# Seeds of a Vandermonde product: factors made at another copy, phases rounded against a constant in PSUM, seeds laid out by power

## The chip, the core and the metric

One core of a Trainium2 chip runs the whole kernel. The core has five engines that each take their instructions in order and wait for one another by semaphores: PE (matmuls; its weight loads are listed apart as PEld), DVE (vector work), ACT (activations and copies), POOL (a second elementwise engine) and SP, which here issues all DMAs. SBUF is the memory on the chip, PSUM the smaller one that PE writes its products to.

The metric is the device time of one execution in microseconds (us), lower is better. Before the change it was 1309.37 us (median of three runs, 1307.53 to 1311.9).

## The reference

Two independent layers read their own inputs; their outputs are joined on the last axis.

```python
# A: a diagonal state space layer, L = 2048, D = 448, N = 256
dt = jnp.exp(log_dt)
A = -jnp.exp(log_A_real) + 1j * A_imag
C = (C_real + 1j * C_imag) * dt[:, None]
P = jnp.exp((A * dt[:, None])[:, :, None] * pos[None, None, :])     # pos = 0 ... 2047
K = 2.0 * jnp.einsum("dn,dnl->dl", C, P).real
y = irfft(rfft(u_t, 2 * L) * rfft(K, 2 * L))[:, :, :L]              # a causal convolution
a = y.transpose(0, 2, 1) + u * D_skip

# B: attention with 16 heads of 28
qkv = (x @ wqkv).reshape(B, S, 3, 16, 28).transpose(2, 0, 3, 1, 4)
p = softmax(q @ k^T * 28 ** -0.5)
b = (p @ v).transpose(0, 2, 1, 3).reshape(B, S, 448) @ wo

out = concatenate([a, b], axis=-1)
```

K[d, l] is a sum over 256 modes of C z^l with z = exp(A dt). The kernel writes l = 64 n1 + n2: per channel it needs two tables of powers of z, called e (64 powers) and g (32 powers, with C in them), and K is their product, summed over the modes on PE.

## The kernel before, in words

The program has two parts.

**The seeds stage** (0 to 239 us of the profile). PE makes q, k and v from x in float32r with a high and a low half. Beside it the function `seeds(o)` (line 314) works through eight groups o of seven channel blocks each: it loads the parameters (`nat`), multiplies them by dt, turns them so that modes lie on partitions (`turn`, into a PSUM tile `pn`), forms 15 multiples of each phase (`phases`: r on DVE, mg on POOL, both 128 x 1680), reduces the phases to half a turn by adding and subtracting a large constant MAGIC (`reduce`: sn = round(r), then r = sn - r), takes sines and cosines on ACT (`sines`) and sizes with Exp (`sizes`), and makes from them: the seeds of e (eight low powers; `places` sets the power 0, `e_all` the others on POOL, into a tile named qhat), the seeds of g (four low powers) and, for each block, the parts of the factors by which the tables are later doubled. All go out to DRAM as `sd`. The list of stages returned at the end of `seeds` is laid over slots, four slots per group; inside this part a scheduler may put instructions of an engine in another order than they are written in.

The tables of ACT hold either Exp or Sin, so a change between them costs a table load (ACT_TABLE_LOAD).

**The loop** (239 to 1275 us): 256 steps, 16 per unit of queries. Here every engine keeps the order in which the program was written. `ORDER` (line 34) sets one step out by hand: m0 to m3 are four products of the row maxima for the unit after (`max_mm`: m0 goes to ACT, m1 to 3 to DVE, which writes mx), s0 to s3 the scores of four heads (`s_mm`, tile pss; ACT takes Exp to p), pv the product with v (tile po), f a slot for other work, v one entry of DVE's queue, k the bookkeeping of the channel blocks, w a slot for wide work. The products of m and f share a ring of three PSUM tiles (pm), so PE can go on only when DVE or ACT has read the one three before.

The 56 channel blocks run through the loop beside attention:

- `load_sd(b)` loads a block's seeds (`sdb`), three blocks ahead.
- `k_seeds(b)` (line 605) is called twice: ACT copies the seeds of e into the table e, some steps later those of g into the table g.
- `k_factors(b)` (line 615): three DVE instructions of 128 x 96 (`fz<-sdb`) multiply sizes by cosines and sines.
- `k_begin` (line 976) starts block b when its due time `K0 + b * KP` (KP = 3.5 steps) has passed and both queues of powers are empty. It copies part of fz into PSUM (`zg`, on ACT) and fills the queues: nine POOL instructions that double e three times (`e_power`, three a step; tiles e and eu), nine entries for DVE that double g (`g_powers`), and a tenth, the factors of block b + 1. DVE takes three entries a step, one of them after k in the step's order.
- From four steps after the start, three f slots multiply e and g (`pm<-e,g`, then `pm<-w,ko`) and send the result to DRAM.

From step 192 on, f slots also run the spectrum: 16 jobs "s" (products with `mw`, elementwise products on DVE, sums on POOL in the tile p, back to DRAM as z), of which the last eight need all 56 blocks, and eight jobs "f" (load zi and ut, `skip` on POOL, four products each, addition on DVE, output). What is left of them behind the last step is interleaved with the last unit's projection. SP issues all loads and stores in program order; a store waits there for its data, and what stands behind it waits too.

Of the kernel before, what the change touches and what calls it, by code (L numbers as in the profile page):

```python
# [8 lines left out]
F32 = mybir.dt.float32  # L9
F32R = mybir.dt.float32r  # L10
I32 = mybir.dt.int32
AF = mybir.ActivationFunctionType
ALU = mybir.AluOpType
# [11 lines left out]
CQ = 512  # L25
# [25 lines left out]
NB = D // 8  # L51
# [3 lines left out]
PO = BO * 8  # L55
LV = 15
NF, NE = 6, 13
F_G = 256
# [3 lines left out]
MAGIC = 1.5 * 2 ** 23  # L62
# [29 lines left out]
def body(ctx, tc, a, out):  # L92
    nc = Engines(tc)
# [4 lines left out]
    def pool(stack, name, bufs=1, space=None, side=None):  # L98
        kw = {} if space is None else {"space": space}
        if side:  # L100
            kw["side"] = side
        return stack.enter_context(tc.tile_pool(name=name, bufs=bufs, reuse_waits="tile", **kw))
# [110 lines left out]
    with ExitStack() as st:  # L213
# [7 lines left out]
        ps_n = pool(st, "ps_n", 2, PSUM)  # L221
# [39 lines left out]
        t = a["A_log_dt"]  # L261
# [6 lines left out]
        half_pi = s_p.tile([128, 1], F32, name="half_pi")  # L268
# [42 lines left out]
        NH = BO * 16  # L311
        mul = lambda e, o_, x_, y_: e.tensor_tensor(o_, x_, y_, ALU.mult)

        def seeds(o):

            q = {}
            vec, pol, act = nc.vector, nc.gpsimd, nc.scalar
# [6 lines left out]
            def times_dt(i):  # L324
                n, d = q["nat"][:, i, :], dt_all[:, i or 4, o:o + 1]
                act.activation(n, n, AF.Copy, scale=d)

            def turn():
                q["ps"] = ps = ps_n.tile([128, CQ], F32, name="pn")[:, :8 * PO].rearrange("p (a b h e) -> p a b h e", a=4, h=2, e=8)
                for i in range(4):  # L330
                    for h in range(2):
                        nc.tensor.transpose(ps[:, i, :, h, :], q["nat"][:, i, h * 128:(h + 1) * 128], ident[:PO, :PO])
                q["tr"] = s_p.tile([128, NH], F32, name="tr", bufs=2)
                act.activation(q["tr"], ps[:, 0].rearrange("p b h e -> p (b h e)"), AF.Copy)
# [10 lines left out]
                mul(pol, mg, lb(q["tr"]), kb(1))  # L345

            def reduce():
                vec.tensor_scalar(q["sn"], q["r"], MAGIC, MAGIC, op0=ALU.add, op1=ALU.subtract)
                vec.tensor_tensor(q["r"], q["sn"], q["r"], ALU.subtract)

            def places():
                se = q_p.tile([128, HG, CQ], F32R, name="qhat", bufs=3).bitcast(F32).rearrange("p h q -> p (h q)")
                q["se"] = se = se[:, :BO * F_G].rearrange("p (b f) -> p b f", f=F_G)
                q["e8"] = se.rearrange("p b (c h e) -> p b c h e", c=2, e=8)
                pol.memset(q["e8"][:, :, 0, :, 0], 1.0)
                pol.memset(q["e8"][:, :, 1, :, 0], 0.0)

            def g_place():
                q["sg"] = sg = s_p.tile([128, BO, SDF - F_G], F32, name="sg", bufs=SGB)
# [15 lines left out]
                both(q["mg"], 0, AF.Exp)  # L375

            def e_all():
                ev = lambda t: t[:, NF:NE].rearrange("p e (b h) -> p b h e", h=16)
                for c, t in enumerate(("r", "sn")):
                    mul(pol, q["e8"][:, :, c, :, 1:], ev(q["mg"]), ev(q[t]))  # L380

            def g_base():

# [29 lines left out]
            def load():  # L413
                if o not in nats:
                    load_nat(o)
                q["nat"] = nats.pop(o)
            dts = lambda *r: [lambda i=i: times_dt(i) for i in r]
            return [[load], [exp_a] + dts(1, 2, 3), dts(0), [turn], [phases], [g_place, reduce], [sines], [sizes, places, g_base],
                    [e_all, g_first], [put_e], [g_copies], [], [put_g]]

        xh, xl = {}, {}
# [177 lines left out]
    sds, egs = {}, {}  # L599
# [5 lines left out]
    def k_seeds(b):  # L605

        if b not in es:
            es[b] = e = g_p.tile([128, 2, 16, N2], F32, name="e", bufs=2)
            nc.scalar.activation(e[:, :, :, :8], sds[b][:, :F_G].rearrange("p (c h e) -> p c h e", c=2, e=8), AF.Copy)
        else:  # L610
            g = g_p.tile([128, 2, 16, N1], F32, name="g", bufs=2)
            nc.scalar.activation(g[:, :, :, :4], sds[b][:, F_G:F_Z].rearrange("p (c h e) -> p c h e", c=2, e=4), AF.Copy)
            egs[b] = es.pop(b), g

    def k_factors(b):
        fzs[b] = fz = g_p.tile([128, 3, 6 * 16], F32, name="fz", bufs=2)
        mg, cs, sn = (sds[b][:, F_Z + 96 * i:F_Z + 96 * i + 96] for i in range(3))
        nc.vector.tensor_tensor(fz[:, 0], mg, cs, ALU.mult)
        nc.vector.tensor_tensor(fz[:, 2], mg, sn, ALU.mult)
        nc.vector.scalar_tensor_tensor(fz[:, 1], mg, -1.0, sn, op0=ALU.mult, op1=ALU.mult)  # L620

    def k_start(b):
        zgs[b] = ps_g.tile([128, CQ], F32, name="zg")
        nc.scalar.activation(zgs[b][:, :Z_G].rearrange("p (f n) -> p f n", f=3), fzs[b][:, :, 48:], AF.Copy)

    def e_power(b, i, q):

        t, m = egs[b][0], 8 << i
        zz = fzs[b].rearrange("p f (k h) -> p k f h", k=6)
        if q == 0:  # L630
            zr = zz[:, i, 0, :][:, None, :, None].to_broadcast([128, 2, 16, m])
            nc.gpsimd.tensor_tensor(t[:, :, :, m:2 * m], t[:, :, :, :m], zr, ALU.mult)
        elif q == 1:
            uts[0] = g_p.tile([128, 2, 16, 32], F32, name="eu")[:, :, :, :m]
            zi = zz[:, i, 1:3, :][:, :, :, None].to_broadcast([128, 2, 16, m])
            nc.gpsimd.tensor_tensor(uts[0], t[:, ::-1, :, :m], zi, ALU.mult)
        else:
            nc.gpsimd.tensor_tensor(t[:, :, :, m:2 * m], t[:, :, :, m:2 * m], uts[0], ALU.add)

    def g_powers(b):  # L640

        t, zg = egs[b][1], zgs[b]
        zz = zg[:, :Z_G].rearrange("p (f k h) -> p k f h", k=3, f=3)
        tt = nc.vector.tensor_tensor

        def first(i, m):
            tt(t[:, :, :, m:2 * m], t[:, :, :, :m], zz[:, i, 0, :][:, None, :, None].to_broadcast([128, 2, 16, m]), ALU.mult)

        def second(i, m, c):
            n = c.stop - c.start  # L650
            u = zg[:, CQ // 2:CQ // 2 + n * 16 * m].rearrange("p (c h m) -> p c h m", c=n, m=m)
            zi = zz[:, i, 1 + c.start:1 + c.stop, :][:, :, :, None].to_broadcast([128, n, 16, m])
            tt(u, t[:, ::-1, :, :m][:, c], zi, ALU.mult)
            return lambda: tt(t[:, c, :, m:2 * m], t[:, c, :, m:2 * m], u, ALU.add)
        both, u = slice(0, 2), {}

        def lowest():
            first(0, 4)
            second(0, 4, both)()
        ops = [lowest, lambda: first(1, 8), lambda: u.update(a=second(1, 8, both)), lambda: u["a"](), lambda: first(2, 16)]  # L660
        for c in (slice(0, 1), slice(1, 2)):
            ops += [lambda c=c: u.update(a=second(2, 16, c)), lambda: u["a"]()]
        return ops
# [196 lines left out]
        max_mm(1, 0, kc)  # L860
    for _ in range(2):
        k_seeds(0)
    k_factors(0)

    urgent, back = collections.deque(), collections.deque()
    powers = {"g": collections.deque(), "e": collections.deque()}
# [109 lines left out]
    def k_begin(s_):  # L976
        if not (k_due and K0 + k_due[0] * KP <= s_ and k_due[0] in egs and not powers["e"] and not powers["g"]):
            return
        b = k_due.popleft()
        k_start(b)  # L980
        powers["g"] += g_powers(b)
        if b + 1 < NB:
            powers["g"].append(lambda: k_factors(b + 1))
        powers["e"] += [lambda i=i, q=q: e_power(b, i, q) for i in range(3) for q in range(3)]
        p0, p1, p2 = k_mm(b)

        def m1():
            p1()
            done["mm"] = b
        m_due.extend((s_ + KD + i, t_) for i, t_ in enumerate((p0, m1, p2)))  # L990
        last[0] = b
# [15 lines left out]
    for s in range(NS):  # L1007
# [26 lines left out]
        ps = []  # L1034
        for op in ORDER:
            if op[0] == "s":
                ps.append(s_mm(u, kt, int(op[1])))
            elif op[0] == "f":
                slot(s)
            elif op == "w":  # L1040
                wide_slot()
            elif op[0] == "v":
                vec()
            elif op == "k":
                k_next()
                k_begin(s)
                for _ in range(1 if s else 2):
                    k_seed(s)
                for _ in range(3):
                    if powers["e"]:  # L1050
                        powers["e"].popleft()()
            elif op == "pv":
                if prev:
                    pv_step(*prev)
                    if prev[1] == NK - 1:
                        fin(prev[0], s)
            elif sm < NS:
                max_mm(sm // NK, sm % NK - more, int(op[1]))
# [80 lines left out]
```

## Time and profile before

| what | us |
|---|---|
| median of three runs (lowest, highest) | 1309.37 (1307.53, 1311.9) |
| the profiled execution, its own time | 1310.93 |
| its span, first to last instruction | 1308.8 |
| PE busy in the span | 1225.8 (94%) |
| DVE busy | 948.6 (72%) |
| ACT busy | 963.7 (74%) |
| POOL busy | 839.0 (64%) |
| granted TensorE clock, mean | 0.98 |

How its lines are read. "L76" stands on every line, since one helper at line 76 records all instructions; the tiles tell them apart. A group reads: line, engine, operation, tile written <- tiles read, partitions x elements written <- read, xcount | busy us, mean ns of one | idle us of the engine just before them, and what ended it. A line of the timeline has start and length in us, engine, operation, tiles, shape and count, then idle time before it. A line of windows has the stretch, its length, busy us of PE, PEld, DVE, ACT and POOL (with the number of instructions), the granted clock, the busy share of the DMA engines and GB/s. A line of waits has the waiting and the awaited engine and tile, us in total, times, and the longest. The chain of waits goes back from the last instruction to what released it, step by step.

### The profile page before, as it was taken

How to read it: one execution, taken by the hardware profiler on the slowest of the kernel's cores; microseconds unless marked ns; L12 is line 12 of the kernel's file. 1: busy time of each engine (PE TensorE's matmuls, PEld its weight loads, DVE VectorE, ACT ScalarE, POOL GpSimd, SP SyncE). 2: the span in 40 equal slices, each digit the busy share in tenths (PEclk: the TensorE clock that was granted, in tenths of full speed). 3: DMA queues.
4: the chain of work that ended last, by engine and by line, in shares of the span. 5: the costliest groups of instructions: out<-in, count | busy, mean ns of one | idle time of the engine just before them, and what ended most of it. 6: DMA issues, size and time to landing. Idle time of an engine off the chain costs nothing.

```text
span 1308.8 us, 32327 instructions
## 1 busy us (share of the span) xinstructions
PE 1225.8 (94%) x12177; PEld 686.0 (52%) x12177; DVE 948.6 (72%) x2194; ACT 963.7 (74%) x2048; POOL 839.0 (64%) x656
## 2 busy tenths in 40 slices
PE   6888976899999999999999999999999999999996
PEld 5666853455555555555555555555555555454332
DVE  5676678878877887777788888888888958453221
ACT  4878873588888888888878888888877657565451
POOL 2455641467777787777788888878879849235341
PEclk9989988899999999999999999999999999999998
DMA  6777779546864545487524225431454533269577
GB/s 195 230 255 267 260 235 294 157 93 153 183 151 105 126 147 167 112 215 196 155 71 95 74 51 136 109 96 39 109 151 124 171 99 107 82 187 287 170 228 192
DMA packets 200084, 205.30 MB, mean 157 GB/s; under 512 B 95992, under 2 KB 158520, under 8 KB 197880
## 3 DMA queue, kind: packets, MB, share of 16 engines
q1 hardware_dynamic: 199928, 203.24, 55.3%
q8 instruction: 96, 1.57, 0.5%
q14 instruction: 60, 0.49, 0.1%
HBM read 120.74 MB, written 82.18 MB: 155 GB/s over the span
## 4 chain that ended last, share of the span: by engine, by line
PE 71%; DVE 8%; DMA 4%; POOL 4%; ACT 3%; issue 2%; SPq 1%; POOLq 0%; DVEq 0%; ACTq 0%
PE pm L76 40%; PE pss L76 16%; PE po L76 16%; DVE mx L76 2%; DMA ut<-in_A_u 2%; POOL p L76 1%; DVE rl L76 1%; ACT tri L76 1%; DVE tri L76 1%; POOL e L76 1%; SPq L76 1%; DVE pr L76 1%; DVE mh L76 1%; ACT sg L76 1%; DVE fz L76 1%
## 5 line engine op out<-in xcount | busy, mean ns | idle before, releaser
L76 ACT ACTIVATE p<-pss 128x512 f32<-128x512 f32 x1024 | 561.9, 610 | 127.9 <-PE pss L76 125.7
L76 DVE TENSOR_REDUCE mx<-pm 128x1 f32<-128x512 f32 x500 | 321.7, 684 | 128.7 <-PE pm L76 127.6
L76 PE MATMUL pss<-qhat,khat 128*128 128x512 f32 x1024 | 403.0, 400 | 0.7 <-ACT p L76 0.6
L76 PE MATMUL pm<-khat,qhat 128*128 128x512 f32 x749 | 330.3, 443 | 9.6 <-DVE mx L76 6.8
L76 POOL TENSOR_TENSOR e<-e,fz 128x256 f32<-128x256 f32 x168 | 203.2, 1209 | 202.3 <-PE pss L76 84.0
L76 PE MATMUL po<-p,v 128*32 128x512 f32 x2048 | 269.8, 594 | 0.0
L76 PEld LDWEIGHTS pm<-khat,qhat 128*128 128x128 f32 x749 | 141.5, 189 | 220.1 <-DVE mx L76 41.5
L76 POOL TENSOR_TENSOR e<-e,eu 128x256 f32<-128x256 f32 x168 | 247.9, 1475 | 13.2
L76 PEld LDWEIGHTS pss<-qhat,khat 128*128 128x128 f32 x1024 | 190.5, 189 | 40.3 <-issue 9.6
L76 POOL TENSOR_TENSOR eu<-e,fz 128x256 f32<-128x256 f32 x168 | 201.7, 1200 | 0.0
L76 DVE CUSTOM_DVE_ANT_0 rl<-pm,rl 128x512 f32<-128x512 f32 x249 | 170.8, 686 | 31.6 <-ACT rl L76 27.3
L76 ACT ACTIVATE rl<-pm 128x512 f32<-128x512 f32 x249 | 151.0, 606 | 19.3 <-PE pm L76 18.9
L76 DVE TENSOR_TENSOR g<-g,zg 128x128 f32<-128x128 f32 x392 | 162.1, 413 | 3.6
L76 POOL TENSOR_TENSOR p<-pr,pr 64x448 f32<-64x448 f32 x64 | 73.3, 1146 | 96.9 <-PE pm L76 61.7
L76 PE MATMUL pm<-xh,khat 112*128 112x512 f32 x256 | 89.0, 430 | 20.6 <-DVE kb L76 7.8
L76 PE MATMUL pm<-kdif,qhat 128*128 128x512 f32 x249 | 102.2, 410 | 4.4 <-DVE pr L76 2.2
L76 DVE TENSOR_TENSOR zg<-g,zg 128x128 f32<-128x128 f32 x224 | 87.7, 392 | 4.7
L76 PEld LDWEIGHTS pm<-e,g 128*32 128x32 f32 x3584 | 58.2, 109 | 45.6 <-issue 23.5
L76 DVE TENSOR_TENSOR pr<-pm,ub 128x448 f32<-128x448 f32 x64 | 36.9, 619 | 53.5 <-PE pm L76 38.7
L76 ACT ACTIVATE y<-pm 128x448 f32<-128x448 f32 x48 | 26.3, 547 | 66.9 <-PE pm L76 44.7
L76 PE MATMUL pm<-e,g 128*32 128x64 f32 x3584 | 73.1, 221 | 1.9 <-POOL e L76 1.9
L76 PEld LDWEIGHTS po<-p,v 128*32 128x32 f32 x2048 | 55.1, 110 | 31.8 <-issue 27.7
(129 smaller groups left out, 1435.6 us busy)
## 6 DMA issues: line engine op xcount, KB each, us to landing
sdb<-sd SPq DMA_DIRECT2D x56, 336.0 KB
khat<-k SPq DMA_DIRECT2D x64, 256.0 KB
qhat<-q SPq DMA_DIRECT2D x64, 256.0 KB
sd<-sg SPq DMA_DIRECT2D x8, 1456.0 KB
k<-hl SPq DMA_DIRECT2D x16, 512.0 KB
q<-hl SPq DMA_DIRECT2D x16, 512.0 KB
v<-v SPq DMA_DIRECT2D x32, 256.0 KB
mw<-in_mw SPq DMA_DIRECT2D x16, 512.0 KB
```

The costliest lines, as they stand in the source:

```text
L76: i = f(*args, **kw)
```

## The change

Four edits.

1. `reduce`: sn is now made by an instruction with a second tensor, a constant MAGIC broadcast from one column of the PSUM tile pn, in place of two immediate constants. The column is written by a small DVE instruction in `turn`.
2. The seeds of e lie in their tile by part (cosine, sine), power and mode, where they lay by part, mode and power. `places`, `e_all` and the copy in `k_seeds` follow.
3. The list of stages: exp_a moves two stages later, the other multiplications by dt accordingly, turn and phases share a stage.
4. `k_factors(b)` is called in `k_seeds` directly after the copy of g's seeds, and is no longer the tenth entry of DVE's queue (nor called ahead of the loop).

```diff
             def turn():
-                q["ps"] = ps = ps_n.tile([128, CQ], F32, name="pn")[:, :8 * PO].rearrange("p (a b h e) -> p a b h e", a=4, h=2, e=8)
+                pn = ps_n.tile([128, CQ], F32, name="pn")
+                q["ps"] = ps = pn[:, :8 * PO].rearrange("p (a b h e) -> p a b h e", a=4, h=2, e=8)
+                q["magic"] = pn[:, 8 * PO:8 * PO + 1]
+                vec.tensor_scalar(q["magic"], half_pi, 0.0, MAGIC, op0=ALU.mult, op1=ALU.add)
...
             def reduce():
-                vec.tensor_scalar(q["sn"], q["r"], MAGIC, MAGIC, op0=ALU.add, op1=ALU.subtract)
+                vec.scalar_tensor_tensor(q["sn"], q["r"], MAGIC, q["magic"][:, :, None].to_broadcast([128, LV, NH]),
+                                         op0=ALU.add, op1=ALU.subtract)
                 vec.tensor_tensor(q["r"], q["sn"], q["r"], ALU.subtract)
...
-                q["e8"] = se.rearrange("p b (c h e) -> p b c h e", c=2, e=8)
-                pol.memset(q["e8"][:, :, 0, :, 0], 1.0)
-                pol.memset(q["e8"][:, :, 1, :, 0], 0.0)
+                q["e8"] = se.rearrange("p b (c e h) -> p c e b h", c=2, e=8)
+                pol.memset(q["e8"][:, 0, 0], 1.0)
+                pol.memset(q["e8"][:, 1, 0], 0.0)
...
             def e_all():
-                ev = lambda t: t[:, NF:NE].rearrange("p e (b h) -> p b h e", h=16)
+                ev = lambda t: t[:, NF:NE].rearrange("p e (b h) -> p e b h", h=16)
                 for c, t in enumerate(("r", "sn")):
-                    mul(pol, q["e8"][:, :, c, :, 1:], ev(q["mg"]), ev(q[t]))
+                    mul(pol, q["e8"][:, c, 1:], ev(q["mg"]), ev(q[t]))
...
-            return [[load], [exp_a] + dts(1, 2, 3), dts(0), [turn], [phases], [g_place, reduce], [sines], [sizes, places, g_base],
+            return [[load], dts(1, 2, 3), [], [exp_a] + dts(0), [turn, phases], [g_place, reduce], [sines], [sizes, places, g_base],
                     [e_all, g_first], [put_e], [g_copies], [], [put_g]]
...
             es[b] = e = g_p.tile([128, 2, 16, N2], F32, name="e", bufs=2)
-            nc.scalar.activation(e[:, :, :, :8], sds[b][:, :F_G].rearrange("p (c h e) -> p c h e", c=2, e=8), AF.Copy)
+            nc.scalar.activation(e[:, :, :, :8], sds[b][:, :F_G].rearrange("p (c e h) -> p c h e", c=2, e=8), AF.Copy)
         else:
             g = g_p.tile([128, 2, 16, N1], F32, name="g", bufs=2)
             nc.scalar.activation(g[:, :, :, :4], sds[b][:, F_G:F_Z].rearrange("p (c h e) -> p c h e", c=2, e=4), AF.Copy)
             egs[b] = es.pop(b), g
+            k_factors(b)
...
     for _ in range(2):
         k_seeds(0)
-    k_factors(0)
...
         powers["g"] += g_powers(b)
-        if b + 1 < NB:
-            powers["g"].append(lambda: k_factors(b + 1))
         powers["e"] += [lambda i=i, q=q: e_power(b, i, q) for i in range(3) for q in range(3)]
```

In the built program the starts of the 56 blocks stand in steps 0, 4, 8 ... 220 before the change, and in steps 0, 4, 7, 11, 14, 18, 21 ... 193 after it; the number of table loads goes from 19 to 17.

## The prediction

> **What bounds the kernel now.** I read the busy time of each engine by stage first, then the same stretches for the scores alone, then waits and the timeline where the change acts.
>
> ```profile
> core 0: us, PE busy (x) PEld busy (x) DVE busy (x) ACT busy (x) POOL busy (x), PEclk, DMA share, GB/s
> 0.00:239.00 239.00, 188.17 (x775) 140.26 (x775) 160.75 (x281) 159.85 (x273) 101.45 (x78) 0.91 0.77 247
> 239.00:652.90 413.90, 411.11 (x4398) 219.59 (x4399) 327.92 (x818) 342.31 (x784) 298.74 (x235) 1.00 0.59 149
> 652.90:963.20 310.30, 307.22 (x3356) 169.64 (x3354) 273.38 (x689) 260.37 (x583) 256.60 (x200) 1.00 0.36 85
> 963.20:1275.50 312.30, 298.35 (x3385) 148.25 (x3385) 181.41 (x395) 196.86 (x403) 175.94 (x141) 1.00 0.53 165
> 1275.50:1308.80 33.30, 20.94 (x268) 8.29 (x268) 5.15 (x14) 4.33 (x8) 6.28 (x3) 0.87 0.73 195
> ```
> ```profile
> 239.00:652.90 413.90, 165.16 (x416) 78.90 (x417) 227.81 (x415) 1.00 0.59 149
> 652.90:963.20 310.30, 138.96 (x353) 66.29 (x352) 193.09 (x353) 1.00 0.36 85
> ```
>
> The second fence is the pss tile alone: four matmuls a step, so 416 and 352 are 104 and 88 steps, 3.98 and 3.53 us each. Three regimes follow. The seeds stage (0 to 239) has no full engine; PE idles 239 - 188.2 = 50.8 us on latency chains. The loop to 963 is PE's: 718 of 724 us busy. After it PE idles 13.9 us in the loop's last 64 steps and 12.4 us behind it. So a gain must come from the first stage, from the end, or not at all; a loss can come anywhere in the middle, where DVE has only (413.9 - 327.9)/104 = 0.83 and (310.3 - 273.4)/88 = 0.42 us idle a step.
>
> **The change, part by part.** *Rounding.* The stage's large instructions, grouped by shape:
>
> ```profile
> L76 DVE TENSOR_SCALAR tri<-tri 128x1680 f32<-128x1680 f32 x8 | 15.7, 1968 | 0.1
> L76 DVE TENSOR_TENSOR tri<-pn,pw 128x1680 f32<-128x1680 f32 x8 | 15.2, 1897 | 0.1
> L76 POOL TENSOR_TENSOR tri<-tr,pw 128x1680 f32<-128x1680 f32 x8 | 24.0, 2998 | 8.1 <-issue 5.8 <-ACT tr L76 2.3
> L76 POOL TENSOR_TENSOR qhat<-tri 128x784 f32<-128x784 f32 x16 | 51.1, 3198 | 0.0
> L76 ACT ACTIVATE e<-sdb 128x256 f32<-128x256 f32 x56 | 24.6, 439 | 3.6 <-DMA sdb<-sd 3.6
> L76 ACT ACTIVATE yk<-pm 128x256 f32<-128x256 f32 x56 | 39.3, 701 | 1.5 <-PE pm L76 1.5
> L76 ACT ACT_TABLE_LOAD x19 | 24.4, 1283 | 1.0 <-PEq L1129 0.7
> ```
> ```profile
> 94.67 1.03 DVE L76 TENSOR_SCALAR tri<-tri 128x1680 f32<-128x1680 f32 x1
> ...
> 173.75 7.64 DVE L76 TENSOR_SCALAR tri<-tri 128x1680 f32<-128x1680 f32 x1
> ```
> ```profile
> 174.05 3.01 POOL L76 TENSOR_TENSOR tri<-tr,pw 128x1680 f32<-128x1680 f32 x1
> 177.01 0.66 POOL L76 TENSOR_TENSOR tri<-tri 128x224 f32<-128x224 f32 x1
> 177.63 2.87 POOL L76 TENSOR_TENSOR qhat<-tri 128x784 f32<-128x784 f32 x1
> ```
> ```profile
> 137.72 3.11 POOL qhat L76
> 149.21 1.28 ACT L76
> 173.75 7.64 DVE tri L76
> 183.68 4.61 PE pm L76 x12
> ```
>
> The rounding takes 1.03 us beside an idle POOL and 7.64 us when POOL runs three instructions back to back: it ends at 181.39, after POOL's last one (180.50). The last fence is the chain of waits: that 7.64 lies on it, with PE's projections behind. The new instruction has an operand in PSUM; the nearest row is the product with pn in PSUM, 1.90 us, never longer. That costs 0.87 us where POOL was quiet and saves 5.7 at the stall. DVE is not full here, so of the dear ones I charge one to the path: -5.7 + 0.9 = -4.8. Bounds: the stall only moves to the subtraction behind it, which still has both inputs in SBUF (+1), or a second chain shortens too (-7).
>
> [...]
>
> *Seeds of e.* POOL takes 3.20 us for 784 elements written 8 apart and read 112 apart, and 3.00 for 1680 contiguous ones. Laid out by power, 784 should cost 784 x 3.00/1680 = 1.40 us (bounds 1.4 and 3.2). It saves 16 x 1.8 = 29 us of POOL, of which one, 1.7 us at 137.72, lies on the chain. The copy of these seeds on ACT now reads 16 elements apart: between 0.44 us (its row) and 0.70 (yk, also 256 elements, written in another order). I take 0.44, as ACT idles 50 of 310 us; the other end is 56 x 0.26 = 14.7 us of ACT.
>
> *Stages.* The built program has 17 table loads for 19; one of 1.28 us lies on the chain at 149.21: -1.3. The small write of the constant, eight times, hides beside PE's transposes. The scheduler sorts this stage anew, which no row prices: I add nothing and keep +10/-8. Sum of the stage: -4.8 - 1.7 - 1.3 = -8, range -16 to +6.
>
> *Factors.* DVE's queue per block loses its tenth entry (the factors), so nine remain at three a step. In the built order blocks start at steps 0, 4, 7, 11, 14 ... 193 and no longer at 0, 4, 8 ... 220: every 3.5 steps. Same work, earlier. Its price is where the factors now stand: in the step before a block starts, ahead of two mx reduces that give PE its buffers back, while POOL still works on the block before.
>
> ```profile
> 810.27 0.41 DVE L76 TENSOR_TENSOR fz<-sdb 128x96 f32<-128x96 f32 x2
> ...
> 810.78 0.68 DVE L76 CUSTOM_DVE_ANT_0 rl<-pm,rl 128x512 f32<-128x512 f32 x1
> ...
> 821.35 0.69 DVE L76 CUSTOM_DVE_ANT_0 rl<-pm,rl 128x512 f32<-128x512 f32 x1 [0.20 <-ACT rl L76]
> ```
> ```profile
> 810.69 0.66 POOL L76 TENSOR_TENSOR e<-e,fz 128x256 f32<-128x256 f32 x1 [2.52 <-ACT rl L76]
> ...
> 820.22 2.38 POOL L76 TENSOR_TENSOR e<-e,eu 128x1024 f32<-128x1024 f32 x1
> ```
> ```profile
> 653.45 2.33 POOL L76 TENSOR_TENSOR e<-e,eu 128x1024 f32<-128x1024 f32 x1
> 653.67 2.40 DVE L76 TENSOR_TENSOR fz<-sdb 128x96 f32<-128x96 f32 x2
> ```
> ```profile
> 980.70 1.34 DVE L76 TENSOR_TENSOR fz<-sdb 128x96 f32<-128x96 f32 x2
> 981.97 1.20 DVE L76 SCALAR_TENSOR_TENSOR fz<-sdb 128x96 f32<-128x96 f32 x1
> ```
>
> At 810 the factors take 0.6 us together because POOL has finished and waits for them (it starts 0.42 us after). At 653 and 980 POOL is busy, and they wait for its instruction to end: 2.0 us there, and 2.5 us from first to last here, for 0.6. Now POOL's run takes 810.69 to 822.60, 11.9 us, so it is busy until 12.3 us after the factors that start it. From one rl of a step to that three steps on (810.78 to 821.35) pass 10.6 us. With blocks three steps apart the next factors meet POOL's last instruction with 1.75 us left, 1.6 us more than now; four steps apart (14.1 us) POOL is done. So one block in two waits 1.6 us. DVE's own idle swallows 0.4. From step 104 to 193 there are 89/7 = 12.7 such pairs: 12.7 x 1.2 = +15 us. Before step 104 three steps take 11.9 us, the wait is 0.4, and DVE's 0.83 idle covers it: 0. Bounds: +4 (a third is felt) and +38 (the first rival).
>
> [...]
>
> *The last part of the loop.* Eight blocks leave the stretch from 963; there PE waited for mx behind such factors (the waits from 963 to 1116: us, times, longest):
>
> ```profile
> PE pm L76 <- DVE mx L76: 4.4, 8, 0.7
> ```
>
> With them POOL's mixture of e and p goes too. Of 13.9 us idle I take back 6 (0 to 10).
>
> *The end.*
>
> ```profile
> 1293.04 1.35 SPq L76 DMA_DIRECT2D ut<-in_A_u  x2
> ...
> 1293.90 0.94 PE L76 MATMUL pm<-ua,on 128*32 128x448 f32 x8
> ...
> 1295.95 10.10 SPq L76 DMA_DIRECT2D out<-ot  x8
> ...
> 1302.74 1.28 DVE L76 TENSOR_TENSOR ot<-pm,ut 128x224 f32<-128x224 f32 x4 [6.32 <-POOL ut L76]
> ```
>
> After the last score PE's order holds 12 of 32 final products now; the last load of ut is queued on SP behind the third projection's output, so it starts at 1293.0 and the last addition at 1302.7; the last output's issue ends at 1306.05, 2.8 us before the span does. In the built order 8 of 32 remain and that load stands ahead of the projections. The end is then the projections (to 1294.84 now), two more products (1.2), an issue of 0.6 and the 2.8 behind it: 1299.4, 24 us behind the last score for 33.3: -9, and +1 for products moved into the loop: -8 (-11 to -4).
>
> Sum: -8 + 15 - 6 - 8 = -7. Against this execution's 1310.9 (span 1308.8 and 2.1 around it) 1303.9; it ran 1.56 above the median of 1309.37, so 1302.
>
> **The rivals.** [...] Place: the three factors ahead of mx. For it: the two rows above, PE at 99%, and DVE with 0.42 us idle a step; against it, in half the blocks POOL is done. It outweighs the 22 us of gains once a block loses 22/55 = 0.4 us on average. If every second block waits 1.6 us, fully felt and before step 104 too, that is 27.5 x 1.6 = 44, less 6 that the early idle hides: 1309.4 - 22 + 38 = 1325.
>
> *No change.* The seeds stage, sorted anew, gives nothing (+8), as its chain runs through loads too: 1310. For it: PE idles there for many releasers; against it, the 7.64 is on the chain.
>
> *Much faster.* POOL, never idle, runs ahead so that factors find it between blocks, and no wait is felt: 1309.4 - 22 = 1287. Against it, POOL cannot start a block before its factors.
>
> [...]
>
> **How the numbers follow.** Forecast 0.40, slower 0.34, no change 0.15, much faster 0.11. A measurement of this kernel tells about 0.3% (4 us) from no change. Faster: 0.9 of the forecast, all of the last and a fifth of no change, 0.50. Same: a tenth of the forecast and 0.6 of no change, 0.13. Slower 0.37. The forecast's own range is 1292 to 1312; both signs hold much, so 1285 to 1328 reaches to the ends.
>
> **What would show it.** Right: roundings all near 1.9 us, the seeds of e near 1.4 on POOL, the loop starting near 231, the first factors near 0.25 and near 1.9 us in turn after step 104, block starts 3 and 4 steps apart, 24 us behind the last score. Wrong: factors of 2 us or more in every block, steps longer than 3.7 us with PE waiting for mx, a loop start at 239 or later, or a subtraction in the seeds stage stalled in place of the rounding.

## The result and the profile after

| | median of four runs (lowest, highest), us | profiled execution, us | its span, us |
|---|---|---|---|
| before | 1309.91 (1307.53, 1311.9) | 1310.9 | 1308.8 |
| after | 1317.74 (1316.83, 1319.04) | 1317.07 | 1315.3 |

After over before is 1.0062, 95% interval 1.0045 to 1.0079: slower by 0.6%. 1302 had been forecast.

The busy time by stage (columns as in the first view of the prediction: stretch, length, busy us of PE, PEld, DVE, ACT and POOL, clock, DMA share, GB/s), of the kernel after, cut at the same steps: the first score, step 104, step 192, the last score.

```profile
0.00:228.70 228.70, 186.87 (x776) 138.69 (x776) 164.25 (x289) 156.84 (x271) 82.25 (x78) 0.94 0.81 258
228.70:655.70 427.00, 421.52 (x4703) 224.86 (x4704) 345.11 (x869) 356.85 (x807) 340.01 (x268) 0.99 0.59 149
655.70:989.80 334.10, 314.78 (x3596) 173.71 (x3594) 301.39 (x734) 272.58 (x602) 295.64 (x230) 0.99 0.34 81
989.80:1291.50 301.70, 288.32 (x2873) 142.47 (x2873) 144.02 (x303) 185.40 (x363) 98.78 (x81) 0.98 0.57 173
1291.50:1315.30 23.80, 18.40 (x237) 7.23 (x236) 3.97 (x10) 4.38 (x8) 3.28 (x2) 0.99 0.50 134
```

Against the stages of before: 228.7 - 239.0 = -10.3, 427.0 - 413.9 = +13.1, 334.1 - 310.3 = +23.8, 301.7 - 312.3 = -10.6, 23.8 - 33.3 = -9.5; together the +6.5 by which the spans differ. The change wins 30 us at the start, the late part and the end, and loses 37 us in steps 0 to 192. There PE also has more to do (421.5 for 411.1 and 314.8 for 307.2, since more blocks fall into these steps), but between steps 104 and 192 it also idles 19.3 us, where it idled 3.1.

The groups of the kernel after that answer to those of before (line, engine, operation, tiles, shapes, count, busy us, mean ns, idle before):

```profile
L76 DVE TENSOR_TENSOR fz<-sdb 128x96 f32<-128x96 f32 x112 | 40.0, 397 | 1.8 <-DMA sdb<-sd 1.8
L76 ACT ACTIVATE e<-sdb 128x256 f32<-128x256 f32 x56 | 37.6, 672 | 3.8 <-DMA sdb<-sd 3.8
L76 POOL TENSOR_TENSOR qhat<-tri 128x784 f32<-128x784 f32 x16 | 29.9, 1877 | 0.0
L76 ACT ACT_TABLE_LOAD x17 | 21.8, 1283 | 1.0 <-PEq L1131 0.7
L76 DVE TENSOR_TENSOR tri<-tri 128x1680 f32<-128x1680 f32 x8 | 20.0, 2496 | 0.1
L76 DVE SCALAR_TENSOR_TENSOR tri<-tri,pn 128x1680 f32<-128x1680 f32 x8 | 15.2, 1900 | 0.2
```

The rounding (last row) takes 1.90 us. The seeds of e take 1.88 us on POOL for 3.20, and their copy on ACT 0.67 for 0.44.

Where the loop loses is seen on the timeline of the kernel after, behind step 104 (start, length, engine, operation, idle time before):

```profile
657.48 1.91 POOL L76 TENSOR_TENSOR e<-e,fz 128x1024 f32<-128x1024 f32 x1
...
658.47 2.92 DVE L76 TENSOR_TENSOR fz<-sdb 128x96 f32<-128x96 f32 x2
...
659.35 1.92 POOL L76 TENSOR_TENSOR eu<-e,fz 128x1024 f32<-128x1024 f32 x1
...
661.31 0.24 DVE L76 SCALAR_TENSOR_TENSOR fz<-sdb 128x96 f32<-128x96 f32 x1
...
661.48 1.28 DVE L76 TENSOR_REDUCE mx<-pm 128x1 f32<-128x512 f32 x2
...
662.21 0.50 PE L76 MATMUL pm<-khat,qhat 128*128 128x512 f32 x1 [2.69 <-DVE mx L76]
```

Two factors of 0.25 us take 2.92, until POOL's instruction ends at 661.27; the two mx stand behind them, and PE waits 2.69 us for the buffer that mx frees. This is the worst one. Of the blocks behind it, up to block 54, every second one's three factors take 1.2 to 1.9 us from first to last, the others 0.6; ahead of step 104 only those of block 16 (1.8) and block 18 (0.8) take longer than 0.6.

And one stall that is no factor's, on the timeline of the kernel after in step 197:

```profile
1007.62 4.77 POOL L76 TENSOR_TENSOR p<-pr,pr 64x448 f32<-64x448 f32 x4 [9.29 <-DMA yk<-yk]
...
1012.48 1.91 POOL L76 TENSOR_TENSOR e<-e,fz 128x1024 f32<-128x1024 f32 x1
...
1014.34 1.91 POOL L76 TENSOR_TENSOR eu<-e,fz 128x1024 f32<-128x1024 f32 x1
1016.33 2.32 POOL L76 TENSOR_TENSOR e<-e,eu 128x1024 f32<-128x1024 f32 x1
1018.70 0.84 PEld L76 LDWEIGHTS pm<-e,g 128*32 128x32 f32 x32 [6.89 <-POOL e L76]
1018.70 1.08 PE L76 MATMUL pm<-e,g 128*32 128x64 f32 x32 [6.46 <-POOL e L76]
```

The last block starts at step 193 now. Its largest doubling stands on POOL behind the sums p of the first spectrum job, and these had waited for their products (POOL idles 9.29 us ahead of them; the DMA named there is not what they read, the products pr that they read end at 1007.5). PE comes to the block's product four steps after its start, as always, and idles 6.46 us. Step 197 takes 13.6 us; those around it 3.4 and 4.3.

### The profile page after: what moved, and what is told of

Same layout as the page of the kernel before. It is cut to its first block, busy times and chain, and to the rows that moved or that the text cites. A ratio compares the mean times of both kernels' runs of the same rounds, so it can differ in the third digit from the quotient of the medians.

```text
span 1315.3 us, 32347 instructions
## 1 busy us (share of the span) xinstructions
PE 1229.9 (94%) x12177; PEld 687.0 (52%) x12177; DVE 958.7 (73%) x2202; ACT 976.0 (74%) x2046; POOL 820.0 (62%) x656
## 4 chain that ended last, share of the span: by engine, by line
PE 69%; DVE 10%; ACT 6%; issue 3%; POOL 2%; DMA 2%; SPq 0%; ACTq 0%; POOLq 0%; DVEq 0%
PE pm L76 38%; PE pss L76 15%; PE po L76 15%; DVE mx L76 3%; DVE fz L76 2%; DVE rl L76 2%; ACT p L76 1%; ACT rl L76 1%; ACT tri L76 1%; DVE g L76 1%; POOL p L76 1%; ACT L76 1%; DMA ut<-in_A_u 1%; ACT sg L76 1%; DVE zg L76 1%
## 5 line engine op out<-in xcount | busy, mean ns | idle before, releaser
L76 PEld LDWEIGHTS pm<-e,g 128*32 128x32 f32 x3584 | 57.0, 110 | 47.9 <-issue 10.7
L76 ACT ACTIVATE ub<-pm 128x224 f32<-128x224 f32 (+1 forms) x96 | 38.6, 448 | 40.5 <-PE pm L76 40.0
```

Source lines behind the costliest of these rows:

```text
L76: i = f(*args, **kw)
```

## The experiments

In all of them the steps and stages are counted as above. Stage times are of one profiled execution of each kernel. Steps 0 to 192, where two kernels have the same program there, agree within 0.1 us (427.0 and 334.1 in the changed kernel, 426.9 and 334.1 in the one with the spectrum job started later); the seeds stage, which nine of the kernels share, ended between 227.5 and 230.5 us.

### Edit 4 out, and edit 4 alone

```diff
 # e1: the changed kernel; e2 is the reverse, on the kernel before
             egs[b] = es.pop(b), g
-            k_factors(b)
...
+    k_factors(0)
...
         powers["g"] += g_powers(b)
+        if b + 1 < NB:
+            powers["g"].append(lambda: k_factors(b + 1))
```

> The changed kernel with edit 4 undone: factors are again the tenth entry of DVE's queue, edits 1 to 3 stay. Theory A (the loss is edit 4's: block starts 3.5 steps apart, with factors that wait for POOL): the loop is as long as before, and only the seeds stage's 10.3 us are gained: 1309.9 - 10.3 = 1299.6 us (1296 to 1304), factors of 0.6 us a block, steps 0 to 192 within 4 us of the 724 us of before. Rival B (the loss is edit 2's: ACT's copy of the seeds of e takes 0.67 us for 0.44, 56 x 0.23 = 13 us): steps 0 to 192 stay 10 us or more longer than before, and the time is 1310 us or more.

> The kernel of before with edit 4 alone. Theory A: the whole of the loop's difference appears, +13.1 and +23.8 in steps 0 to 104 and 104 to 192, -10.5 and -9.6 behind: 1309.9 + 16.8 = 1326.7 us (1321 to 1331). Rival B (the copy on ACT has a large part in it): 13 us less of it, 1309 to 1317 us.

Measured: edits 1 to 3 without 4 take 1304.86 us, 0.9968 (0.9956 to 0.9981) of before; edit 4 alone 1320.46 us, 1.0088 (1.0069 to 1.0107). So the loss is edit 4's, and the two add up to the change: -0.3% and +0.9%. With edit 4 alone steps 104 to 192 take 333.6 us, as after the whole change, although ACT's copy is the short one there: the copy is not the cause (B falls for them). Theory A missed both ranges, by 0.9 and by 0.5 us. The first time the seeds stage gives 10.7 us (it ends at 228.3), but steps 0 to 192 take 728.9 us, 4.7 more than before.

### The layout of e's seeds out as well

The edit takes the six lines of edit 2 out of the former kernel, as they stand in the diff of the change.

> Edits 1 and 3 alone: rounding against the constant in PSUM and the new list of stages, with factors in the queue and the seeds of e laid out as before. Theory G (with edits 1 to 3 the loop was 4.9 us longer than before, 1041.4 for 1036.5, because ACT's copy of e's seeds is 0.23 us longer in each block; POOL's seeds of e are worth 1 to 3 us in the seeds stage): 1304.9 - 4.9 + 2 = 1302 us (1299 to 1304), the loop within 2 us of 1036.5. Rival H (the copy costs nothing, the 4.9 us come from elsewhere, and the layout is worth what POOL saves): 1305 to 1309 us.

Measured: 1305.61 us, 0.9982 (0.9966 to 0.9999); edit 2 is worth nothing that these runs can tell. By stage it is two effects: the seeds stage ends at 232.5 us with the old layout and at 228.3 with the new one, -4.2 (2.0 to 5.0 with the spread of the seeds stage given above); steps 0 to 192 take 725.8 with the old one and 728.9 with the new one, +3.1, with a copy of 0.44 and of 0.67 us. Theory G had the loop's side right, H the total; the gain on POOL was larger than G's 1 to 3 us, unless the spread made it so. (The late part of this run was 4.0 us longer than that of edits 1 to 3, with one step of 8.6 us near the end, which stays unexplained.)

### Factors without a wait, twice

```diff
 # e3; zg is one fixed tile here, mgp its free columns 144 to 239 in PSUM
         if b not in es:
             es[b] = e = g_p.tile([128, 2, 16, N2], F32, name="e", bufs=2)
+            nc.scalar.activation(mgp, sds[b][:, F_Z:F_Z + 96], AF.Copy)
...
-        mg, cs, sn = (sds[b][:, F_Z + 96 * i:F_Z + 96 * i + 96] for i in range(3))
+        cs, sn = (sds[b][:, F_Z + 96 * i:F_Z + 96 * i + 96] for i in (1, 2))
+        mg = mgp
 # e9: as e3, but
+            if b == 0:
+                nc.scalar.activation(mgp, sds[b][:, F_Z:F_Z + 96], AF.Copy)
```

> The changed kernel, with the sizes that all three factor instructions read copied to PSUM by ACT (one more ACT instruction of 128 x 96 a block, about 0.3 us), so that none has two inputs in SBUF. Block starts stay 3.5 steps apart. Theory A1 (the waits of the factors make the loss): no factor above 0.35 us, PE's idle time in steps 104 to 192 falls from 19.3 to below 7 us, and the time falls by the factors' excess, 49.5 - 56 x 0.6 = 16 us: 1302 us (1297 to 1307). Rival C (what makes the loss is the cadence itself: PE has 18 us more to do in these steps and DVE, ACT and POOL no slack, the waits are swallowed): 1313 to 1318 us.

> The changed kernel with the sizes that the three factor instructions read kept in PSUM, copied there for the first block alone (all blocks use its sizes, so the tables hold other numbers), so that no ACT instruction is added and no factor has two inputs in SBUF. All three instructions stay, in their place. Theory P (their place ahead of two mx reduces costs by itself; with four steps a block and no wait the step of the factors took 4.18 us for 3.67): factors of 0.6 us in every block, steps 104 to 192 take 312.4 us (without factors) + 25 x 0.5 = 325, steps 0 to 104 about 427, in all 1292.4 + 12.5 + 3.4 = 1308 us (1304 to 1312). Theory A1 (only the waits for POOL cost): steps 104 to 192 below 316 us, 1292 to 1297 us.

In both, every block's factors take 0.6 us from first to last: with one input in PSUM none of them waits for POOL. But the first one took 1327.05 us, 1.0139 (1.0121 to 1.0157), outside both theories. Its groups show why it can't be read for the question:

```profile
L76 ACT ACTIVATE zg<-sdb 128x96 f32<-128x96 f32 x56 | 14.3, 256 | 30.2 <-ACT ko L76 20.6 <-issue 3.9 <-DMA sdb<-sd 3.8
```

The added copies are 14.3 us of ACT, and ACT idles 30.2 us ahead of them: the cure brought its own wait, in the order of ACT. The second one, which differs only in leaving out these copies but for the first, took 24.5 us less: 1302.57 us, 0.9954 (0.9939 to 0.9968), 15.2 below the changed kernel. Its stages 2 and 3:

```profile
229.70:655.90 426.20, 421.38 (x4702) 224.42 (x4703) 344.46 (x869) 357.00 (x807) 338.89 (x268) 0.99 0.59 149
655.90:977.10 321.20, 313.14 (x3595) 173.18 (x3594) 287.08 (x734) 271.44 (x601) 293.66 (x230) 1.00 0.35 85
```

The waits cost 334.1 - 321.2 = 12.9 us behind step 104 and 0.8 ahead of it. That is not all: A1 falls, P had the kind right and took 325 for 321.2. The time lies between the two ranges, 1.4 us below P's.

### No factors in the loop

```diff
-            k_factors(b)
+            if b < 2:
+                k_factors(b)
+            else:
+                fzs[b] = fzs[b - 2]
```

> The changed kernel, with factors made for the first two blocks alone; all later blocks use these two again (three DVE instructions a block are left out, so the tables hold other numbers). Starts stay 3.5 steps apart. Theory A1 (the factors' waits on DVE are the loss in the middle): steps 104 to 192 fall from 334 to 316 us (310.3 and 3.1 blocks more x 1.95 us of PE), steps 0 to 104 from 427 to 422: 1317.7 - 23 = 1295 us (1290 to 1300). Rival C (it is the cadence: POOL, ACT and DVE have too much in 3.5 steps, and PE waits for them somewhere else): steps 104 to 192 stay above 327 us, 1310 us or more.

Measured: 1292.40 us, 0.9873 (0.9856 to 0.9890). Its stages 2, 3 and 4:

```profile
229.90:653.60 423.70, 420.50 (x4703) 225.10 (x4704) 330.54 (x785) 356.42 (x806) 338.86 (x268) 0.99 0.59 150
653.60:966.00 312.40, 309.39 (x3595) 174.20 (x3594) 274.98 (x659) 270.79 (x601) 295.68 (x232) 1.00 0.36 87
966.00:1266.50 300.50, 287.67 (x2873) 142.19 (x2873) 143.69 (x301) 185.36 (x363) 97.88 (x80) 0.99 0.57 174
```

Rival C falls: a start every 3.5 steps costs nothing by itself. Against before, stage 2 has 420.5 - 411.1 = 9.4 us more for PE and is 9.8 longer, stage 3 2.2 more and 2.1 longer, and stage 4 10.7 less: for the most part work moved, not added. (About 3.1 of the 9.8 + 2.1 us are ACT's longer copy, by edits 1 to 3 with and without edit 2.) Against the run without waits, the factors' own time, 0.6 us a block, makes 321.2 - 312.4 = 8.8 us in stage 3 and 426.2 - 423.7 = 2.5 in stage 2. PE's waits in stage 3 say how much of this is idle time ahead of mx (us, times, longest; the changed kernel, without waits, without factors):

```profile
PE pm L76 <- DVE mx L76: 19.2, 17, 2.7
```
```profile
PE pm L76 <- DVE mx L76: 6.6, 16, 0.9
```
```profile
PE pm L76 <- DVE mx L76: 1.0, 5, 0.2
```

That is 12.6 of the 12.9 us of the waits, and 5.6 of the 8.8 of the own time. The rest of the 8.8 goes with a longer busy time of PE (313.1 us for 309.4 with the same products), whose cause stays open.

### The place of the factors

```diff
 # e5
-K0, KP, KD, UP = 0, 3.5, 4, 3
+K0, KP, KD, UP = 0, 4, 4, 3
 # e12: k_seeds only notes b in f_due; at the end of the step, behind the loop over ORDER
+        if f_due:
+            k_factors(f_due.pop())
```

> The changed kernel with KP = 4 in place of 3.5: factors stay at the copy of g's seeds, blocks start every four steps again. Theory C (the cadence makes the loss, by the waits or by the load on the engines): all factors near 0.6 us, steps 104 to 192 back to 311 to 316 us, and the time that of edits 1 to 3 without edit 4, 1304.9 us (1301 to 1308). Rival P (the place of the factors ahead of two mx reduces costs by itself, whatever the cadence: 0.6 us of DVE in one step, where it has 0.42 us to spare, felt once a block): 56 x 0.3 us more, 1318 to 1325.

> The changed kernel with the three factor instructions at the end of the step, behind its last entry of DVE's queue, where the kernel of before had them; starts stay 3.5 steps apart. Theory P (the place ahead of two mx reduces is what makes their own 0.6 us felt): the 8.8 us of steps 104 to 192 and the 2.6 us before go, the waits for POOL stay: steps 104 to 192 near 325 us, 1306 us (1303 to 1310). Rival Q (any place on DVE costs as much at this cadence, as the next mx pair stands behind them in either case, and POOL is as busy there): steps 104 to 192 at 332 us or more, 1315 to 1322 us.

With four steps a block the time was 1340.69 us, 1.0234 (1.0213 to 1.0256): outside both ranges, worse than P, although POOL is done when most factors come, and the factors of 49 of the 56 blocks take 0.6 us. Against edits 1 to 3 with the same starts, where the factors are the tenth entry of the queue, at the end of a step, stage 2 takes 422.8 for 416.8, stage 3 323.6 for 312.1, stage 4 326.5 for 312.5. The last 14.0 are mostly waits for POOL again: six blocks' factors take 2.4 us in stage 4, in either run, but here PE waits for the mx behind them (this run, then the factors at the end of a step):

```profile
PE pm L76 <- DVE mx L76: 14.6, 9, 2.5
```
```profile
PE pm L76 <- DVE mx L76: 4.5, 8, 0.7
```

The 6.0 and 11.5 us of stages 2 and 3 hold one such block, at step 104, which takes 8.4 us for 7.2; all the others there take 0.6. The timeline of this run at one block shows the mechanism without any wait for POOL:

```profile
670.38 0.39 PE L76 MATMUL pm<-khat,qhat 128*128 128x512 f32 x1
...
670.62 0.42 DVE L76 TENSOR_TENSOR fz<-sdb 128x96 f32<-128x96 f32 x2
...
670.96 0.25 DVE L76 SCALAR_TENSOR_TENSOR fz<-sdb 128x96 f32<-128x96 f32 x1
...
671.12 1.28 DVE L76 TENSOR_REDUCE mx<-pm 128x1 f32<-128x512 f32 x2
...
671.86 0.50 PE L76 MATMUL pm<-khat,qhat 128*128 128x512 f32 x1 [0.38 <-DVE mx L76]
```

The product is done at 670.77, its mx starts at 671.12, behind the factors, and PE waits 0.38 us for it. The step of this block takes 4.18 us, the same step with factors at the end of the one before 3.67.

With starts 3.5 steps apart the end of the step is no cure: 1314.94 us, 1.0049 (1.0032 to 1.0066), 2.8 us below the changed kernel, stage 3 at 333.7. Stage 2, where hardly any factor waits, gains 2.2 us, nearly the whole 2.5 of their own time; but the waits of the factors stay (1.3 to 2.0 us in every second block behind block 30, 3.9 in block 30 itself), and stage 3 gains nothing. Rival Q holds for stage 3; the time is at the lower edge of its range. What the factors' own time costs there at the step's end without the wait wasn't tried.

### The stall of step 197

```diff
 # e4: the job and its loads later
-            f_ready["s", 0], f_ready["s", 1] = s, NS
+            f_ready["s", 0], f_ready["s", 1] = s + 4, NS
 # e8: loaded as before, started later
-        due = max(f_ready.get((kind, f), 0), s_ + FL[kind])
+        due = max(f_ready.get((kind, f), 0), s_ + FL[kind] + (4 if (kind, f, i) == ("s", 0, 0) else 0))
```

> The changed kernel, with the first spectrum job held back by four steps (ready at step 196 in place of 192). Theory D (step 197 takes 13.6 us because the last block's largest doubling stands on POOL behind the sums of the second spectrum job, which wait for their products): step 197 takes 4 to 5 us, the time falls by 6 to 9 us: 1309 to 1312. Rival E (the spectrum work sets the end, so what is held back comes back there): 1317 to 1325 us.

> The changed kernel, with the first spectrum job loaded as before but started four steps later. With the job and its loads held back the time fell by 3.6 us, and step 196 took 10.6 us, as its first product waited 4.2 us for the load of mw. Theory D (one stall of 9 us, POOL's last doubling behind the sums): no step from 190 to 200 above 6 us, 1317.7 - 9 = 1309 us (1307 to 1311). Rival E (what is held back comes back in the last part, as PE is busy there): 1313 to 1318 us.

Measured: 1314.15 us (1.0041, 1.0030 to 1.0052) and 1307.99 us (0.9989, 0.9979 to 0.9998). In the first the stall changed its kind: step 196 takes 10.6 us there, as PE waits 4.2 us for the job's load of mw, which SP issues at 1003.4 only, behind a store of on and four loads of q; the time lies between the two theories. In the second no step from 190 to 200 is above 4.8 us, and its stage 4 is 10.8 us shorter than the changed kernel's:

```profile
988.50:1279.40 290.90, 285.26 (x2873) 140.72 (x2873) 144.16 (x304) 184.97 (x363) 98.04 (x80) 1.00 0.58 177
```

D holds: of the 10.8 us only 1.2 come back, behind the last score (25.0 us for 23.8).

### A version that is faster than both

```diff
 # e10, in seeds(o); in the loop fzs[b] is a view of sdb and k_factors is gone
+            def f_all():
+                f = q["f"]
+                mul(pol, f[:, 2], f[:, 0], f[:, 2])
+                mul(pol, f[:, 0], f[:, 0], f[:, 1])
+                act.activation(f[:, 1], f[:, 2], AF.Copy, scale=-1.0)
...
-                    [e_all, g_first], [put_e], [g_copies], [], [put_g]]
+                    [e_all, f_all, g_first], [put_e], [g_copies], [], [put_g]]
 # e11: the due time of e8 as well
```

> The changed kernel with the factors made in the seeds stage, for seven blocks at once (two POOL products of 128 x 672 and one ACT copy a group), and stored in place of sizes, cosines and sines; the loop has no factor instruction left. Theory P/W (place and waits of the factors cost 25 us in the loop, POOL's idle 146 us of the seeds stage hide the new ones): the loop as without factors, 1292.4 us, and 0 to 6 us more in the seeds stage: 1292 to 1299. Rival S (the new instructions stand on the chain of each group): 8 x 2.5 us more in the seeds stage, 1310 us.

> The same, and the first spectrum job started four steps later, as in the run that took step 197 from 13.6 to 3.7 us. If both are causes apart, the gains add: 9.7 us below the run with the factors in the seeds stage, 1283 to 1290 us. If the loop without factors has no such stall, nothing more is gained.

Measured: 1296.84 us, 0.9915 (0.9896 to 0.9933), and with the later spectrum job 1290.32 us, 0.9863 (0.9847 to 0.9880), 19.6 below the median of before and 27.4 below the change. The factors cost 234.3 - 229.9 = 4.4 us more in the seeds stage than leaving them out (6.1 in the second run), and the first time is within its range. The second missed its range by 0.3 us: the gain is 6.5 us by the medians, against 9.7 expected; it is 9.9 in stage 4, but its seeds stage ended 1.7 us later and its end took 1.3 longer. The stages of the last version:

```profile
0.00:236.00 236.00, 188.93 (x776) 139.55 (x776) 157.90 (x289) 162.51 (x279) 106.24 (x94) 0.93 0.78 250
236.00:660.00 424.00, 420.77 (x4703) 225.12 (x4703) 329.31 (x779) 356.60 (x806) 338.84 (x268) 0.99 0.59 150
660.00:972.40 312.40, 309.44 (x3595) 174.26 (x3594) 275.01 (x659) 270.79 (x601) 295.75 (x232) 1.00 0.36 87
972.40:1263.10 290.70, 285.08 (x2873) 140.81 (x2873) 143.85 (x301) 184.85 (x363) 96.59 (x78) 1.00 0.58 178
```

From 236 to 972 PE is busy 730.2 of 736.4 us: the loop is PE's again, with starts 3.5 steps apart.

## Why the prediction was wrong

The whole change, by where its us went (stages of the runs above; "moved" is the run without factors against before, "own time" the run without waits against that, "waits" the changed kernel against that):

| | predicted | measured |
|---|---|---|
| seeds stage | -8 | -10.3 |
| waits of the factors for POOL | +15 | 0.8 + 12.9 = +13.7 |
| own time of the factors | 0 | 2.5 + 8.8 = +11.3 |
| block work moved into steps 0 to 192, with some 3.1 of ACT's longer copy | 0 | 9.8 + 2.1 = +11.9 |
| late part of the loop, without the stall | -6 | 290.9 - 312.3 = -21.4 |
| stall of step 197 | 0 | +10.8 |
| end | -8 | -9.5 |
| sum | -7 | +6.5 |

**The step that failed** is the one on edit 4: "Same work, earlier. Its price is where the factors now stand", where only the wait was priced. Two terms were left out. The first is the factors' own 0.6 us. I took it as moved from one place of DVE's queue to another at no cost, though the same paragraph named the place, "ahead of two mx reduces that give PE its buffers back", and the part before it had DVE's idle time as an average of 0.42 us a step. That average isn't at the place: with four steps a block and no wait for POOL, 0.38 us of the 0.6 came through to PE (the row at 671.86), and in steps 0 to 192 of the change the own time cost 11.3 us. The second is the meeting in step 197: earlier starts put the last block's largest doubling and the first spectrum sums on POOL at the same time. I had written that POOL's mixture of e and p goes with the blocks that leave; one such meeting was left, the dearest of all, 10.8 us.

**The waits** were right in kind and place: one block in two, from block 30 on, little ahead of step 104 (0.8 us), 13.7 us for 15. That the size came out is in part luck. The 13 waiting blocks' factors take 22.7 us for 7.7, so a wait is 1.2 us on average and not 1.6; but 12.9 of these 15.0 us are felt, so DVE's idle time took up 0.2 us of a wait and not 0.4: the average idle time of a step misled here as well. In the two runs with one input of the factors in PSUM none of them waited for POOL: 0.25 us for one on average, 0.6 us for the three in every block.

**The shift of work** was not in the sum either, but by itself it costs nothing: of the 11.9 us, all but the copy's 3.1 move from later parts into the steps ahead of them. I took -6 there for idle time alone; the same stage without the stall fell by 21.4, of which 298.35 - 285.26 = 13.1 are PE's busy time and 8.3 its idle time. The two errors, 11.9 and 15.4, cancel within 4 us.

**The seeds stage.** The rounding came out as worked out, 1.90 us in all eight. The bound named there, a stall of the subtraction instead, came true in part. The subtraction had one long stall before the change and has two after it, on the timelines of the kernel before and after:

```profile
86.28 4.68 DVE L76 TENSOR_TENSOR tri<-tri 128x1680 f32<-128x1680 f32 x1
```
```profile
79.90 3.00 POOL L76 TENSOR_TENSOR tri<-tr,pw 128x1680 f32<-128x1680 f32 x1 [2.79 <-ACT tr L76]
...
80.95 3.72 DVE L76 TENSOR_TENSOR tri<-tri 128x1680 f32<-128x1680 f32 x1
...
118.23 3.00 POOL L76 TENSOR_TENSOR tri<-tr,pw 128x1680 f32<-128x1680 f32 x1 [2.50 <-issue]
...
118.59 4.41 DVE L76 TENSOR_TENSOR tri<-tri 128x1680 f32<-128x1680 f32 x1
```

the two after it by one POOL instruction each, not by three in a row, and the stage gained all the same. Rounding and subtraction together took DVE 35.2 us, for 34.1 before: the quiet roundings lost nearly what the stalled one won, and the subtraction took 1.6 more. Edits 1 and 3 gave 239.0 - 232.5 = 6.5 us of the stage (6.1 predicted), edit 2 gave 4.2 (1.7 predicted). Whether the rounding or the list of stages gave the 6.5 no run tells, so that it is near the 4.8 + 1.3 of the forecast does not show its account to be right. The seeds of e cost 1.88 us on POOL, not the 1.40 worked out from a row. (Before the change they were written in runs of seven neighbours, 8 apart from run to run, not singly 8 apart as the prediction has it; only the reads were 112 apart.) ACT's copy took 0.67 us, near the end of its bounds that I didn't take, yet only 3.1 of its 56 x 0.23 = 13 us were felt.

**The end** was right: 23.8 us for 24, the last load of ut stands ahead of the last score, and the last output is issued 2.7 us before the span ends:

```profile
1290.07 1.32 SPq L76 DMA_DIRECT2D ut<-in_A_u  x2
...
1309.89 0.94 PE L76 MATMUL pm<-zi,wb 128*32 128x224 f32 x16
...
1311.32 1.25 SPq L76 DMA_DIRECT2D out<-ot  x2
```

**The rivals.** The slower one, with 1.6 us of wait in every second block, felt in full, had the sign, but not the mechanism: hardly any wait was felt before step 104 (0.8 us), and behind it they came as in the forecast; what it lacked is the same own time and the same stall. Its 1325 is 7 above what was measured. The rival of no change fell with the 10.3 us of the seeds stage, the much faster one with the 13.7 us of waits.

## What to carry to other kernels

An instruction that moves in an in-order queue can have a price at its new place even when it waits for nothing (here 0.38 us of PE's time for 0.6 us of factors): look at what stands directly behind it and who waits for that, not at the engine's mean idle time. When a chain of work is made to end earlier, look up what starts at that time on each engine that it shares. And where a small job costs in a full loop at each place tried for it, make it in bulk in a stage that has an idle engine: here the factors cost 4.4 to 6.1 us in the seeds stage, where they took 25 us of the loop.

## What the runs showed of the hardware

A long stall of PE can be paid twice. The windows around step 197 and around the factor at 658 in the kernel after (last three columns: granted clock, DMA share, GB/s):

```profile
1012.00:1018.50 6.50, 0.24 (x2) 0.00 (x0) 0.70 (x2) 1.50 (x4) 6.34 (x4) 0.68 0.00 0
1018.50:1020.50 2.00, 1.80 (x40) 1.15 (x44) 0.00 (x0) 0.22 (x1) 0.15 (x1) 0.50 0.04 8
1020.50:1022.50 2.00, 2.00 (x24) 0.69 (x16) 0.00 (x0) 0.00 (x0) 0.00 (x0) 0.50 0.00 0
1022.50:1024.50 2.00, 2.00 (x12) 1.30 (x5) 0.69 (x1) 0.81 (x2) 0.00 (x0) 0.50 0.00 0
1024.50:1026.50 2.00, 2.00 (x42) 1.35 (x44) 1.09 (x2) 1.85 (x5) 0.00 (x0) 0.97 0.33 115
```
```profile
664.20:666.20 2.00, 2.00 (x8) 1.17 (x5) 0.91 (x2) 0.43 (x2) 1.84 (x4) 0.50 0.08 23
666.20:668.20 2.00, 2.00 (x42) 1.37 (x44) 1.79 (x6) 2.00 (x5) 1.92 (x3) 0.99 0.00 0
```

Behind 6.46 us of idling the clock is 0.50 until about 1024.5, some 6 us in which eight products of po take 1.93 us (at 1019.55), where the next eight take 1.04 (at 1026.21): by estimate, from half the clock in these 6 us, 3 us more, lost while it is shown as busy. Behind only 2.69 us of idling (to 662.21) it falls to 0.50 too, until about 666. In the kernel before it stayed at 1.00 behind 1.89 us (to 655.84), and in the kernel after behind nine waits for mx of 1.25 to 1.49 us (to 689.70 the first, to 979.30 the last).
